# Loading the last piece of the output weight in two DMAs, three rows and then one, in a decode attention kernel

## The chip, the cores and the metric

The kernel runs on one core of one Trainium2 chip. PE is TensorE, DVE VectorE and ACT ScalarE; SP (SyncE) issues the DMAs. A landing is the update of a semaphore by one of the sixteen DMA engines when its share of a transfer has arrived. The metric is the device time of one execution in microseconds (us); the span that the profile shows is some 1.8 us shorter (185.9 for 187.7). A ratio below is the mean time of one kernel's fast runs over that of the other's of the same rounds, so it is not quite the ratio of the medians that are quoted beside it.

## The reference

One decoding step of attention over the last 512 positions of a key and value cache, with 32 query heads on 8 key and value heads, and a projection at each end:

```
q = x @ wq                       # x [32, 1, 512], wq [512, 4096]
k, v = last 512 rows of k_cache, v_cache, each head repeated 4 times
p = softmax(q k^T / sqrt(128))
out = (p v) @ wo                 # wo [4096, 512], bf16
```

The caches' window is 67 MB, wq and wo are 4 MB each. Everything is read once.

## The kernel before

SP issues all large loads in one order: wq, the tiles of K and V (2 MB each), then wo in eight pieces of 512 KB. A piece holds 512 rows of wo; each of the 128 partitions takes four neighbour rows, which are 4 KB in one run of memory. The pieces lie where wq and parts of the attention's data were before, so they wait for a PV stage (the product p v of the reference) to be done with that memory, and come last in the queue:

```python
sp.wait_ge(pe_PV, 2 * Z_HOME.rindex("w") + 2)
for hg in range(NHG):                                  # NHG = 8
    sp.dma_start(
        wo_sb[:, hg].rearrange("p i n -> p (i n)"),
        wo[hg * 512:(hg + 1) * 512, :].rearrange("(m i) n -> m (i n)", i=4),
    ).then_inc(sem_wo[hg], 16)
sp.wait_ge(dve_out, 2)
sp.wait_ge(act_out, 2)
sp.dma_start(out..., out_sb...).then_inc(sem_out, 16)
```

PE takes the pieces in the same order. Each piece is sixteen matmuls: four rows for each partition (i), four column groups (c) that share the array:

```python
for hg in range(NHG):
    pe.wait_ge(sem_wo[hg], 16)
    for i in range(4):
        for c in range(4):
            ins = pe.matmul(
                X_ps[32 * c:32 * (c + 1), 2, 0:128],
                lhsT=o_sel[:, i, hg, :],
                rhs=wo_sb[:, hg, i, c * 128:(c + 1) * 128],
                start=(hg == 0 and i == 0), stop=(hg == NHG - 1 and i == 3),
                tile_position=(0, 32 * c),
            )
ins.then_inc(pe_fin, 1)
```

After the last matmul DVE and ACT copy two quarters of the result each, and SP stores it.

Of the kernel before, what the change touches and what calls it, by code (L numbers as in the profile page):

```python
# [12 lines left out]
def bass_standalone__sliding_block_cached__sampling_kernel(  # L13
# [7 lines left out]
):  # L21
    B, Sq, D = x.shape
    _, HKV, SK, DH = k_cache.shape
    HD = wq.shape[1]
    HQ = HD // DH
# [16 lines left out]
    NHG = HQ // 4  # L42
    NBG = 4 * G
    SELCUT = B - 8
    RING = 3
    XD = 20
    ZD = XD // 4
    ZA = (NBG - XD) // 4
    DMA_ORDER = (
# [21 lines left out]
    with ExitStack() as es:  # L71
        sb = lambda name, shape, dt: es.enter_context(nc.sbuf_tensor(name, shape, dt))
        ps = lambda name, shape, dt: es.enter_context(nc.psum_tensor(name, shape, dt))
        sem = lambda name: es.enter_context(nc.semaphore(name))
# [7 lines left out]
        P_bf = sb("P_bf", [P, KS, KR], BF16)  # L82
        PTc = sb("PTc", [P, RING, KR, REP], BF16)
        pick = sb("pick", [P, REP, KS + P], BF16)
# [20 lines left out]
        wo_sb = w_sb[:, :, :].rearrange("p k n -> p (k n)").rearrange("p (g i n) -> p g i n", g=NHG, i=4)  # L105
# [14 lines left out]
        sem_x = sem("sem_x")  # L120
        sem_wq = [sem(f"sem_wq{i}") for i in range(2)]
        sem_wo = [sem(f"sem_wo{i}") for i in range(NHG)]
        sem_k = [sem(f"sem_k{i}") for i in range(NK)]
        sem_v = [sem(f"sem_v{i}") for i in range(NV)]
        sem_out = sem("sem_out")
# [45 lines left out]
        def z_of(q):  # L171
            return {"w": Z_w, "k": Z_k, "t": Z_t}[Z_HOME[q]]

        def z_waits(eng, q):
            if q == 0:
                eng.wait_ge(pool_mask, 3)
                eng.wait_ge(pe_q, 1)
            elif Z_HOME[q] in Z_HOME[:q]:
                eng.wait_ge(pe_PV, 2 * Z_HOME[:q].rindex(Z_HOME[q]) + 2)
            elif Z_HOME[q] == "k":  # L180
                eng.wait_ge(dve_T, 2 * NCH - 2)
            else:
                eng.wait_ge(pe_S, NQUAD)

        def cache_rows(cache, m):
            q, e = divmod(m, 2)
            rows = cache[4 * q:4 * q + 4, :, SK - W:, :].rearrange("b g (s r) d -> (b g) s (r d)", s=KS)
            return rows[:, :, e * CR * DH:(e + 1) * CR * DH]

        @block.sync  # L190
        def _(sp):
            sp.dma_start(
                w_sb[:, 2:4, :].rearrange("p k n -> p (k n)"), wq_rows[:, wq_half:]
            ).then_inc(sem_wq[1], 16)
            for name in DMA_ORDER:
                n = int(name[1:])
                if name[0] == "K":
                    if n >= NK:
                        sp.wait_ge(dve_T, 2 * (n - NK + 1))
                    sp.dma_start(  # L200
                        K_sb[:, n % NK].rearrange("p r d -> p (r d)"), cache_rows(k_cache, n)
                    ).then_inc(sem_k[n % NK], 16)
                else:
                    if n >= NV:
                        sp.wait_ge(pe_PV, n - NV + 1)
                    sp.dma_start(
                        V_sb[:, n % NV].rearrange("p r d -> p (r d)"), cache_rows(v_cache, n)
                    ).then_inc(sem_v[n % NV], 16)
            sp.wait_ge(pe_PV, 2 * Z_HOME.rindex("w") + 2)
            for hg in range(NHG):  # L210
                sp.dma_start(  # L211
                    wo_sb[:, hg].rearrange("p i n -> p (i n)"),
                    wo[hg * 512:(hg + 1) * 512, :].rearrange("(m i) n -> m (i n)", i=4),
                ).then_inc(sem_wo[hg], 16)
            sp.wait_ge(dve_out, 2)
            sp.wait_ge(act_out, 2)
            sp.dma_start(
                out.rearrange("b s n -> b (s n)"), out_sb[:, :, :].rearrange("b c n -> b (c n)")
            ).then_inc(sem_out, 16)
            sp.wait_ge(sem_out, 16)  # L220
# [58 lines left out]
        def _(pe):  # L279
# [104 lines left out]
            for hg in range(NHG):  # L384
                pe.wait_ge(sem_wo[hg], 16)
                for i in range(4):
                    for c in range(4):
                        ins = pe.matmul(
                            X_ps[32 * c:32 * (c + 1), 2, 0:128],
# [5 lines that stand above are left out]
# [3 lines left out]
        def _(dve):  # L398
# [44 lines left out]
            def spread(q, part):  # L443
# [3 lines left out]
                for k in range(ZD * part, ZD * (part + 1)):  # L447
                    ins = dve.tensor_scalar(  # L448
                        z_of(q)[:, k].rearrange("p x r -> p (x r)"),
                        PTc[:, q % RING].rearrange("p x r -> p (x r)"),  # L450
                        mask[:, k:k + 1], None, op0=ALU.mult,
# [25 lines left out]
        def _(act):  # L477
# [23 lines left out]
            def pt_evac(q):  # L501
                act.wait_ge(pe_PT, q + 1)
                if q >= RING:
                    act.wait_ge(dve_Z, q - RING + 1)
                    act.wait_ge(act_Z, q - RING + 1)
                act.activation(  # L506
                    PTc[:, q % RING], PT_ps[:, :, :].rearrange("p r x -> p x r"), ACTF.Copy
                ).then_inc(act_PT, 1)

            def spread(q, part):  # L510
                if part == 0:
                    act.wait_ge(act_PT, q + 1)
                    z_waits(act, q)
                for k in range(XD + ZA * part, XD + ZA * (part + 1)):
                    ins = act.activation(  # L515
# [57 lines left out]
```

## Time and profile before

| | before |
|---|---|
| time, median of the first 3 runs | 187.70 us (187.68 to 187.76) |
| span of the profiled run | 185.9 us |
| DMA engines, mean rate over the span | 408 GB/s |
| last landing of wo | 182.90 us |
| last matmul's end | 183.38 us |

How to read it: DMA is busy all through, the compute engines are not. The page's lines on DMA add what kinds of packets there are (the counts "under" a size include the semaphore packets of 4 bytes) and, for the issues, how many there were, their size and the median us from issue to landing:

```profile
DMA packets 6160, 75.80 MB, mean 408 GB/s; under 512 B 704, under 2 KB 768, under 8 KB 1792
...
w_sb<-in_wo_dram SPq DMA_DIRECT2D x8, 512.0 KB, 20.3
```

The 1792 less 768 are the 1024 packets of 4 KB of wo: 8 pieces, 128 partitions.

### The profile page before, as it was taken

To read this page: it belongs to the slowest core of one execution; us is meant where nothing else is said; L and a number is where in the kernel's file an instruction comes from. 1 tells how busy PE (TensorE), PEld (TensorE's weight loads), DVE (VectorE), ACT (ScalarE), POOL (GpSimd) and SP (SyncE) were. 2 spreads that over 40 slices of the span, in tenths; PEclk is the share of its full clock that TensorE was granted. 3 is DMA by queue.
4 is the path that set the end of the run, shared out by engine and by line. 5 is a ranking of instruction groups with operands and counts; after the bars stand their busy time and mean duration, and the time that the engine had idled before them with its cause. 6 is when DMAs were issued, how large, how long until landed. Compare 5 with 4: busy or idle time off the path is not lost.

```text
span 185.9 us, 3841 instructions
## 1 busy us (share of the span) xinstructions
PE 110.3 (59%) x1604; PEld 90.7 (49%) x1604; DVE 131.8 (71%) x239; ACT 82.4 (44%) x142; POOL 32.1 (17%) x82
## 2 busy tenths in 40 slices
PE   0232004346179925949726992459699975999851
PEld 0100001032069804929326881129669974999741
DVE  0006999689999799985899959999999993010001
ACT  3001000259420199011992039826989999711011
POOL 7100390500700071050420060000030000000000
PEclk9999999999999995796955899657999999699999
DMA  6999999999999999999999999999999999999980
GB/s 208 419 444 423 430 430 419 444 423 426 426 419 430 426 419 430 434 419 434 418 430 430 423 434 412 441 430 416 432 416 430 423 430 426 423 430 404 401 326 25
DMA packets 6160, 75.80 MB, mean 408 GB/s; under 512 B 704, under 2 KB 768, under 8 KB 1792
## 3 DMA queue, kind: packets, MB, share of 16 engines
q1 hardware_dynamic: 6096, 75.53, 96.2%
q8 instruction: 12, 0.20, 0.4%
q10 hardware_dynamic: 48, 0.03, 0.1%
q14 instruction: 4, 0.03, 0.0%
HBM read 75.53 MB, written 0.03 MB: 406 GB/s over the span
## 4 chain that ended last, share of the span: by engine, by line
DMA 58%; DVE 22%; PE 11%; issue 4%; SPq 3%; ACT 0%; DVEq 0%
DMA V_sb<-in_v_cache_dram 31%; DVE KT_sb L426 14%; DMA w_sb<-in_wo_dram 12%; DMA K_sb<-in_k_cache_dram 8%; PE O_ps L353 7%; DMA w_sb<-in_wq_dram 6%; DVE w_sb L448 4%; DVE QA_sb L416 2%; PE S_ps L316 2%; SPq L211 2%; PE X_ps L296 1%; PE PT_ps L335 1%; SPq L200 1%; DVE oT_sb L409 0%; DVE KT_sb L404 0%
## 5 line engine op out<-in xcount | busy, mean ns | idle before, releaser
L426 DVE STREAM_TRANSPOSE KT_sb<-K_sb 128x2048 uint32<-128x2048 uint32 x32 | 72.3, 2287 | 1.2 <-DMA K_sb<-in_k_cache_dram 1.1
L353 PE MATMUL O_ps<-w_sb,V_sb 128*128 128x128 bf16 x640 | 46.1, 241 | 10.5 <-DMA V_sb<-in_v_cache_dram 5.6
L353 PEld LDWEIGHTS O_ps<-w_sb,V_sb 128*128 128x128 bf16 x640 | 44.7, 109 | 13.7 <-issue 7.0
L265 POOL COPY QBD<-QA_sb 32x64 bf16<-32x64 bf16 x64 | 25.6, 540 | 79.6 <-PE S_ps L316 62.0
L515 ACT ACTIVATE w_sb<-PTc,mask 128x512 bf16<-128x512 bf16 x60 | 38.9, 729 | 0.0
L316 PE MATMUL S_ps<-KT_sb,QBD 128*32 128x512 bf16 x256 | 20.9, 479 | 26.3 <-DVE KT_sb L426 19.8
L448 DVE TENSOR_SCALAR w_sb<-PTc,mask 128x512 bf16<-128x512 bf16 x100 | 30.2, 370 | 4.9 <-PE O_ps L353 4.9
L316 PEld LDWEIGHTS S_ps<-KT_sb,QBD 128*32 128x32 bf16 x256 | 7.8, 110 | 35.9 <-issue 32.0
L487 ACT ACTIVATE X_ps<-S_ps,negmax 128x512 f32<-128x512 f32 x8 | 5.3, 659 | 42.2 <-DVE negmax L435 42.2
L335 PE MATMUL PT_ps<-P_bf,pick 128*128 128x128 bf16 x128 | 11.8, 265 | 18.0 <-ACT P_bf L496 14.7
L335 PEld LDWEIGHTS PT_ps<-P_bf,pick 128*128 128x128 bf16 x128 | 10.2, 122 | 20.9 <-ACT P_bf L496 16.3
L525 ACT ACTIVATE oT_sb<-O_ps 128x128 bf16<-128x128 f32 x8 | 6.0, 750 | 26.0 <-PE O_ps L353 26.0
L515 ACT ACTIVATE K_sb<-PTc,mask 128x512 bf16<-128x512 bf16 x24 | 15.3, 717 | 1.6 <-DVE KT_sb L426 1.6
L353 PE MATMUL O_ps<-K_sb,V_sb 128*128 128x128 bf16 x256 | 15.1, 217 | 1.3 <-DMA V_sb<-in_v_cache_dram 1.0
L353 PEld LDWEIGHTS O_ps<-K_sb,V_sb 128*128 128x128 bf16 x256 | 14.5, 96 | 2.1 <-issue 1.3
L448 DVE TENSOR_SCALAR K_sb<-PTc,mask 128x512 bf16<-128x512 bf16 x40 | 12.1, 377 | 0.3 <-ACT PTc L506 0.2
L353 PE MATMUL O_ps<-KT_sb,V_sb 128*128 128x128 bf16 x128 | 9.1, 240 | 2.4 <-DMA V_sb<-in_v_cache_dram 2.4
L353 PEld LDWEIGHTS O_ps<-KT_sb,V_sb 128*128 128x128 bf16 x128 | 8.9, 108 | 2.5 <-issue 2.5
L469 DVE CAST K_sb<-S_ps 128x256 bf16<-128x256 f32 x1 | 0.4, 424 | 12.7 <-PE S_ps L365 12.7
L515 ACT ACTIVATE KT_sb<-PTc,mask 128x512 bf16<-128x512 bf16 x12 | 7.8, 725 | 0.0
L467 DVE CAST K_sb<-X_ps 128x384 bf16<-128x384 f32 x1 | 0.6, 558 | 9.8 <-PE X_ps L365 9.8
L496 ACT ACTIVATE P_bf<-X_ps,recip 128x512 bf16<-128x512 f32 x8 | 5.5, 685 | 4.4 <-DVE recip L441 4.4
(41 smaller groups left out, 49.5 us busy)
## 6 DMA issues: line engine op xcount, KB each, us to landing
K_sb<-in_k_cache_dram SPq DMA_DIRECT2D x16, 2048.0 KB, 15.2
V_sb<-in_v_cache_dram SPq DMA_DIRECT2D x16, 2048.0 KB, 17.0
w_sb<-in_wq_dram SPq DMA_DIRECT2D x2, 2048.0 KB, 9.7
w_sb<-in_wo_dram SPq DMA_DIRECT2D x8, 512.0 KB, 20.3
oT_sb<-in_x_dram ACTq DMA_DIRECT2D x1, 32.0 KB, 4.5
out_dram<-oT_sb SPq DMA_DIRECT2D x1, 32.0 KB, 1.5
```

The source lines that it names most:

```text
L211: sp.dma_start(wo_sb[:, hg].rearrange("p i n -> p (i n)"), wo[hg * 512:(hg + 1) * 512, :].rearrange("(m i) n -> m (i n)", i=4),).then_inc( ...
L265: pool.tensor_copy(dst[:, i, :, x0:x0 + 4], src).then_inc(pool_qbd, 1)
L316: ins = pe.matmul(S_ps[32 * c:32 * c + 32, q % 2, :], lhsT=QBD[:, q % 2, g, b, e, :], rhs=bass.AP(tensor=KT_sb, offset=s0 * slot + (b * G ...
L335: ins = pe.matmul(PT_ps[:, r, :], lhsT=pick[:, r, KS - s:KS - s + P], rhs=P_bf[:, s, :], start=(s == 0), stop=(s == KS - 1), tile_position ...
L353: ins = pe.matmul(O_ps[:, q % 2, 0:P], lhsT=V_sb[:, m % NV, r, :], rhs=z_of(q)[:, :, x0 + r, :], start=(e == 0 and r == 0), stop=(e == 1 a ...
L416: dve.tensor_copy(QA[32 * a:32 * a + 32, c], QW[32 * c:32 * c + 32, :, :, a::4].rearrange("p h k q -> p h q k"),).then_inc(dve_q, 1)
L426: dve.transpose(KT_w[:, n % NK, b].rearrange("p i r s -> p r i s"), K_w[:, n % NK, :, 32 * b:32 * b + 32],).then_inc(dve_T, 1)
L448: ins = dve.tensor_scalar(z_of(q)[:, k].rearrange("p x r -> p (x r)"), PTc[:, q % RING].rearrange("p x r -> p (x r)"), mask[:, k:k + 1], N ...
L487: act.activation(P_f32, S_ps[:, q % 2, :], ACTF.Exp, bias=negmax[:, q:q + 1], scale=SCALE, accum_out=sums[:, q:q + 1],).then_inc(act_exp, 1)
L496: act.activation(P_bf[:, :, :], P_f32.rearrange("p (x s) -> p s x", s=KS), ACTF.Copy, scale=recip[:, q:q + 1],).then_inc(act_P, 1)
L515: ins = act.activation(z_of(q)[:, k].rearrange("p x r -> p (x r)"), PTc[:, q % RING].rearrange("p x r -> p (x r)"), ACTF.Copy, scale=mask[ ...
L525: act.activation(oT_sb[:, :, 4 * q:4 * q + 4].rearrange("p h a -> p a h"), O_ps[:, q % 2, 0:P].rearrange("p (a h) -> p a h", a=4), ACTF.Co ...
```

## The change

The intent is to leave less for PE to do after the last byte has landed. The last piece comes as three rows for each partition (384 KB), then one row (128 KB) under a semaphore of its own. PE works on the first three rows while the last one is still coming. The constant `WO_CUT = 3` and the semaphore `sem_last` are new; the rest is this:

```diff
             for hg in range(NHG):
-                sp.dma_start(
-                    wo_sb[:, hg].rearrange("p i n -> p (i n)"),
-                    wo[hg * 512:(hg + 1) * 512, :].rearrange("(m i) n -> m (i n)", i=4),
-                ).then_inc(sem_wo[hg], 16)
+                for i0, i1 in ((0, 4),) if hg < NHG - 1 else ((0, WO_CUT), (WO_CUT, 4)):
+                    sp.dma_start(
+                        wo_sb[:, hg, i0:i1].rearrange("p i n -> p (i n)"),
+                        wo[hg * 512:(hg + 1) * 512, :].rearrange("(m i) n -> m (i n)", i=4)[:, i0 * 512:i1 * 512],
+                    ).then_inc(sem_last if i0 else sem_wo[hg], 16)
 ... (PE)
                 for i in range(4):
+                    if hg == NHG - 1 and i == WO_CUT:
+                        pe.wait_ge(sem_last, 16)
```

More of the change, by code (lines that the diff above doesn't have):

```diff
@@ L45, in bass_standalone__sliding_block_cached__sampling_kernel @@
     RING = 3
+    WO_CUT = 3
     XD = 20
@@ L122, in bass_standalone__sliding_block_cached__sampling_kernel @@
         sem_wo = [sem(f"sem_wo{i}") for i in range(NHG)]
+        sem_last = sem("sem_last")
         sem_k = [sem(f"sem_k{i}") for i in range(NK)]
```

## The prediction

> **What bounds the kernel now.** I read the page's slices first, then the chain that ended last, then the timeline of the last microseconds, then busy time by stretch over the same microseconds.
>
> The slices say that the DMA engines are full from the second slice to the last but one, at some 420 GB/s, whatever the compute engines do:
>
> ```profile
> DMA  6999999999999999999999999999999999999980
> GB/s 208 419 444 423 430 430 419 444 423 426 426 419 430 426 419 430 434 419 434 418 430 430 423 434 412 441 430 416 432 416 430 423 430 426 423 430 404 401 326 25
> ```
>
> So the kernel is a stream of 75.5 MB, and its end is the landing of the last piece in that stream plus what has to follow it. The end of the chain shows which piece, and what follows (columns: start us, length us, what):
>
> ```profile
> 159.94 22.96 DMA w_sb<-in_wo_dram
> 182.90 0.04 issue
> 182.94 0.44 PE X_ps L388 x16
> 183.38 0.02 issue
> 183.40 0.28 DVE oT_sb L472
> 183.68 0.31 DVEq L71
> ```
>
> The last piece of wo (512 KB) lands at 182.90; then sixteen matmuls, two evictions and the store of the result run one after the other, and the span closes at 185.9. The change touches the first two of these links alone. The timeline shows how PE lives in that stretch:
>
> ```profile
> 180.48 0.41 PE L388 MATMUL X_ps<-w_sb,K_sb 128*32 128x128 bf16 x16 [0.51 <-DMA w_sb<-in_wo_dram]
> 181.70 0.41 PE L388 MATMUL X_ps<-w_sb,K_sb 128*32 128x128 bf16 x16 [0.82 <-DMA w_sb<-in_wo_dram]
> 182.94 0.41 PE L388 MATMUL X_ps<-w_sb,K_sb 128*32 128x128 bf16 x16 [0.83 <-DMA w_sb<-in_wo_dram]
> ```
>
> The last three pieces come 1.22 and 1.24 us apart, PE needs 0.41 us for each and is idle 0.83 us before each: it waits for the landing and for nothing else. The stretches say how few DMA engines are still at it (columns: busy us of PE, PEld, DVE, ACT, POOL, then the granted clock, the DMA share and GB/s):
>
> ```profile
> 179.00:180.00 1.00, 0.97 (x72) 0.80 (x60) 0.00 (x0) 0.00 (x0) 0.00 (x0) 1.00 0.76 303
> 181.00:182.00 1.00, 0.30 (x16) 0.23 (x16) 0.00 (x0) 0.00 (x0) 0.00 (x0) 1.00 0.21 86
> 182.00:183.00 1.00, 0.17 (x12) 0.06 (x8) 0.00 (x0) 0.00 (x0) 0.00 (x0) 1.00 0.06 25
> ```
>
> A share of 0.06 is one engine of sixteen. The records of single landings in the trace agree: of the sixteen engines' shares of the last piece, thirteen have landed by 181.66, the other three at 182.68, 182.89 and 182.90. So the last landing is set by one or two slow engines, each of which carries 8 rows of 4 KB of every wo piece, one behind the other. I therefore reckon with one engine, not with 420 GB/s.
>
> **What the Trainium skill says.** (1) "DMA: Bandwidth & Descriptors", section "Why a DMA increments its semaphore by 16 and not by 1": each engine that takes part adds one to the semaphore behind its own data, and only the full 16 means that all has landed. The trace agrees: PE starts at 182.94, after the sixteenth update at 182.90, although thirteen were there 1.24 us earlier. (2) The same page, "Why small descriptors are slow (HBM only)": a fixed overhead of about three cycles for each packet. The trace allows a check. On one engine that works alone the packets of 4096 bytes follow each other every 155.4 ns, those of 16384 bytes every 611 ns; the difference is 455.6 ns for 12288 bytes, so 0.0371 ns a byte, and 155.4 - 4096 x 0.0371 leaves 3.5 ns of fixed cost. It is as small as the page says. (3) "Perfetto Trace Analysis", "DMA Optimizations": transfers under 2 KB have significant overhead, and splitting may let work start sooner where the engines are idle. Here both apply at once: the new last packets have 1 KB. The trace speaks against a large overhead: the 1 KB packets of the result's store and of the load of x mostly take 44 to 47 ns. (4) "Runtime: NRT & Kernel Launch", "Instruction fetch mechanics": instructions come in blocks of 16 KB by the sequencer's own DMA queue. The trace has twelve such packets, each of 1.01 to 1.10 us on one engine. Between landings just before and just after those at about 151.8, 163.2 and 171.8 us, one more engine each time is behind the rest by about 1 us more. These are the likely makers of the three stragglers, which is my inference.
>
> **The change part by part.**
>
> *Bytes and issues.* The last 512 KB go as 384 KB (three rows of wo, 3 KB for each partition) and 128 KB (one row, 1 KB). The bytes and the engines stay. Added are one DMA issue on SP, 8 packets and one semaphore packet for each engine, and one wait on PE; nothing is removed.
>
> *Landing of the last byte.* On the slow engine: before, 8 packets of 155.4 ns and one semaphore packet of about 6 ns, so 1.249 us (measured from the slowest landing of one piece to that of the next: 1.24). After, 8 packets of 3 KB at 3072 x 0.0371 + 3.5 = 117.5 ns, a semaphore packet of 6, 8 packets of 1 KB at 41.5 ns, a semaphore packet of 6: 0.940 + 0.006 + 0.332 + 0.006 = 1.284 us. The last landing comes 0.035 us later, at about 182.94. The 384 KB land 0.34 us before it, at about 182.60.
>
> *PE.* Twelve matmuls (three rows, four column groups each) start at about 182.64. Windows cut through the last group show how it fills: the first 4 matmuls are over 0.24 us after the start, 8 after 0.29, 12 after 0.35, 16 after 0.41. So the twelve are through at about 182.99, and have been issued by about 182.84, ahead of the last landing: they lie wholly beside the transfer. After the last landing 4 matmuls are left, 0.24 us in place of 0.41. The term is -0.17 us. It can't be more by this change, as most of the 0.24 is the way of one matmul through the array (219 ns is the record of each).
>
> *The extra wait on PE.* It stands before the four and is already being waited at when the last semaphore comes; the old wait in front of the sixteen had the same place on the path. 0.
>
> *The extra issue on SP.* An issue of wo takes 0.43 us, but the eighth took 8.57 us, from 159.94 to 168.51: something in the queue was full. The ninth may have to wait likewise, for one more 2 MB piece of V to land (V's last two land at 167.9 and 172.8). That puts it at some 173.4 us. The fastest engine gets to the last rows at about 179. The slack is over 5 us, so 0 on the path.
>
> *What follows.* The evictions, the store and the 1.8 us between the span (185.9) and the time (187.7) stay.
>
> *Sum:* +0.035 - 0.17 = -0.135 us. 187.70 - 0.135 = 187.565, told as 187.57 us.
>
> **Rivals.**
>
> *The small packets cost much more than 41.5 ns.* For it: in the load of x some first packets of 1 KB took 179 to 361 ns, and the skill warns of transfers under 2 KB. Against it: those are the first in an empty queue, and the ones behind them took 44 to 47; here the queue is full. If each of the eight took 75 ns, the landing would be 0.27 us later on top, and the time 187.83.
>
> *The ninth issue is late and leaves a gap.* For it: the 8.57 us issue. Against it: the slack above. If it did come after 182.6, the last row would need its whole way from issue to landing, of which the shortest here is the store's 1.5 us: about 189.2. A chance of some 3 in 100.
>
> *The gain is hidden by the stragglers moving.* The end hangs on which engines carry the late instruction fetches. Twelve whole fetches serve PE's stream, and the change adds a single instruction near its end, so the fetches ahead should stay where they are. If one fetch went to another engine, the end would move by up to 1 us either way: 186.6 to 188.6. For it: any new instruction or semaphore could shift the program. A chance of 4 in 100.
>
> *Nothing at all.* If the 4 matmuls took as long as the 16 after a wait (the array filling anew), the time would be 187.74. Against it speaks the 0.24 us of the first four in the same group.
>
> **Range and chances.** The sum has an uncertainty of about 0.06 us in its two terms. The three runs before lie within 0.08 us, and another session or chip may shift by about as much. This gives 187.57 with 187.40 to 187.75 for 8 in 10. A change of 2% is 3.75 us, more than all that follows the last landing (3.0 us), so faster by over 2% is nearly out of the question: 0.005. Slower by over 2% needs a stall larger than any named here: 0.005. Within 2%: 0.99.
>
> **What would show it.** In the changed profile: PE idle once more between a group of 12 and a last group of 4 of L388; the last group some 0.24 us long; about 0.3 us between the two landings; the page's packets under 2 KB up by 128 plus 16 semaphore packets; the distance from the last landing to the span's end down from 3.0 to about 2.85 us. The step on packets is wrong if the last landing is over 0.1 us later than before. The step on SP is wrong if the DMA share falls to 0 before the last landing. The whole prediction is wrong if the set of engines that land after the others changes, which would show as a move of all wo landings by 0.3 us or more.

## The result

The changed kernel took 187.62 us (median of 6 runs, 187.49 to 187.99), the kernel before 187.75 us (median of 6, 187.68 to 187.95). The ratio is 0.9995 with a 95% interval from 0.9982 to 1.0008: the same. The difference of the medians, 0.13 us, is what was predicted, but with single runs that spread over 0.5 us the times alone can't show that it is more than chance. The profile can, because it shows the few links that the change touches.

First the slices of the changed kernel, DMA share and GB/s. They are as before, up to noise:

```profile
DMA  6999999999999999999999999999999999999980
GB/s 194 434 448 412 437 423 423 448 412 437 420 416 441 416 427 434 416 437 427 423 421 423 441 423 420 434 423 430 428 412 434 427 423 430 420 423 411 405 332 27
DMA packets 6304, 75.80 MB, mean 408 GB/s; under 512 B 720, under 2 KB 912, under 8 KB 1936
```

The packets under 2 KB went from 768 to 912: 128 packets of 1 KB and 16 semaphore packets. Of the last microsecond ahead of the last landing there is, as before, only a small share (0.09 here, 0.06 before):

```profile
182.00:183.00 1.00, 0.45 (x24) 0.18 (x12) 0.00 (x0) 0.00 (x0) 0.00 (x0) 1.00 0.09 31
```

That is the work of three engines: by the packet records they write until 182.46, 182.50 and 182.51, and nothing moves after that, as these records end 0.4 to 0.5 us ahead of the landings.

Then the end of the chain (start us, length us, what) and PE's timeline of the last two pieces:

```profile
182.67 0.04 issue
182.71 0.59 PE X_ps L393 x16
183.30 0.02 issue
183.32 0.28 DVE oT_sb L477
```

```profile
181.75 0.41 PE L393 MATMUL X_ps<-w_sb,K_sb 128*32 128x128 bf16 x16 [0.82 <-DMA w_sb<-in_wo_dram]
...
182.71 0.56 PE L393 MATMUL X_ps<-w_sb,K_sb 128*32 128x128 bf16 x16 [0.55 <-DMA w_sb<-in_wo_dram]
```

The chain merges the last sixteen matmuls into one piece that begins at 182.71. It looks longer than before (0.59 for 0.44 us), but it begins earlier against the stream, and it holds a wait. Windows cut at the two landings take it apart (columns as in the prediction):

```profile
182.67:182.99 0.32, 0.28 (x12) 0.18 (x12) 0.00 (x0) 0.00 (x0) 0.00 (x0) 1.00 0.00 0
182.99:183.30 0.31, 0.28 (x12) 0.10 (x4) 0.00 (x0) 0.00 (x0) 0.00 (x0) 1.00 0.00 0
```

Between the two landings PE loads twelve weights, after the second one four. The rest of PE's time in the second window is the end of the twelve, which by their records were still in the array.

A fixed point is needed to compare the two profiles, as the whole stream comes some hundredths or tenths earlier or later from run to run. The landing of the seventh piece serves, as nothing up to it is changed. In the trace's records of landings, the slowest engine's share of each piece came, in us:

| | seventh piece | three rows | last of wo | last matmul's end | seventh to end |
|---|---|---|---|---|---|
| before | 181.66 | | 182.90 | 183.38 | 1.72 |
| changed | 181.71 | 182.67 | 182.99 | 183.30 | 1.59 |

So the last byte comes 1.28 in place of 1.24 us after the seventh piece, and the last matmul ends 0.31 in place of 0.48 us after the last byte: +0.04 and -0.17, together -0.13 us. The ends of matmuls are modelled by the profile, but the copy on DVE, which waits for the last one, says the same: it begins 0.50 us after the last landing before (183.40) and 0.33 us after it here (183.32). There is one profile of before; of the changed kernel there is a second in e1.

### The profile page after: what moved, and what is told of

It is laid out like the page before. It is cut to its first block, busy times and chain, and to the rows that moved or that the text cites. A ratio compares the mean times of both kernels' runs of the same rounds, so it can differ in the third digit from the quotient of the medians.

```text
span 185.9 us, 3842 instructions
## 1 busy us (share of the span) xinstructions
PE 109.0 (59%) x1604; PEld 89.4 (48%) x1604; DVE 131.9 (71%) x239; ACT 82.3 (44%) x142; POOL 32.0 (17%) x82
## 4 chain that ended last, share of the span: by engine, by line
DMA 64%; DVE 20%; PE 9%; issue 3%; SPq 3%; DVEq 0%
DMA V_sb<-in_v_cache_dram 31%; DMA K_sb<-in_k_cache_dram 14%; DMA w_sb<-in_wo_dram 12%; DVE KT_sb L431 12%; PE O_ps L356 8%; DMA w_sb<-in_wq_dram 6%; DVE w_sb L453 4%; DVE QA_sb L421 2%; SPq L214 2%; PE X_ps L299 1%; SPq L202 1%; DVE oT_sb L414 0%; DVE KT_sb L409 0%; PE X_ps L393 0%; DVE maxv L438 0%
## 5 line engine op out<-in xcount | busy, mean ns | idle before, releaser
L356 PE MATMUL O_ps<-w_sb,V_sb 128*128 128x128 bf16 x640 | 47.0, 244 | 9.6 <-DVE w_sb L453 5.0
L356 PEld LDWEIGHTS O_ps<-w_sb,V_sb 128*128 128x128 bf16 x640 | 45.6, 110 | 12.3 <-DVE w_sb L453 6.5
L356 PE MATMUL O_ps<-KT_sb,V_sb 128*128 128x128 bf16 x128 | 7.5, 217 | 2.3 <-DMA V_sb<-in_v_cache_dram 2.3
L356 PEld LDWEIGHTS O_ps<-KT_sb,V_sb 128*128 128x128 bf16 x128 | 7.3, 96 | 2.5 <-issue 2.5
L409 DVE CAST KT_sb<-X_ps 128x512 bf16<-128x512 f32 x1 | 0.7, 692 | 9.2 <-PE X_ps L299 9.2
```

The source lines that it names most:

```text
L356: ins = pe.matmul(O_ps[:, q % 2, 0:P], lhsT=V_sb[:, m % NV, r, :], rhs=z_of(q)[:, :, x0 + r, :], start=(e == 0 and r == 0), stop=(e == 1 a ...
```

## The experiments

All kernels gave correct results. The kernel before ran beside them on the same chip. Experiments e1 to e8 were made on one chip and share its runs of before: median 187.89 us over the 11 runs beside the first set (e1 to e4), and 187.86 over 12 for the second (e5 to e8), which are the same 11 and one more; they lie between 187.59 and 188.30. That is a wider spread than the result's, and the second set is compared almost wholly with runs that were made some minutes earlier. All single runs here count as in the fast state; e9 and e10 are one run each, on another chip, of unknown state.

My theory was the sum in the prediction: two small terms at the end of the stream, and nothing else. The main rivals: packets of 1 KB or a further DMA cost much more; the wait comes back in another form; the late instruction blocks decide.

### e1: the changed kernel again

> The changed kernel once more, as the control of this set. My theory: 0.135 us less than before, so a ratio of 0.9993, too small to be told from 1 by five rounds in which single runs spread over 0.2 to 0.5 us. In the profile, from the slowest landing of the seventh wo piece to the end of the last matmul: 1.59 us (before: 1.72). Rival (a wait has taken the place of the work removed): 1.70 us or more.

Measured: 187.61 us (187.47 to 188.35), ratio 0.9989, interval 0.9973 to 1.0005. The end of its chain:

```profile
182.74 0.59 PE X_ps L393 x16
183.33 0.02 issue
```

The seventh piece landed at 181.73, so the distance to the last matmul's end is 1.60 us, as predicted. The two landings of the last piece came at 182.70 and 183.01, 1.28 us after the seventh. The profile repeats to 0.01 us what the times can't resolve.

### e2 and e5: the split transfer without the gain on PE

```diff
-                    if hg == NHG - 1 and i == WO_CUT:
+                    if hg == NHG - 1 and i == 0:
                         pe.wait_ge(sem_last, 16)
```

> The split transfer alone: PE waits for both parts before the last sixteen matmuls, so nothing is gained on PE. My theory: landing of the last row 1.28 us after the slowest landing of the seventh piece (before 1.24), then the whole group of 0.41 us again: 1.76 us from that landing to the last matmul's end, 0.04 above before and 0.17 above the change. Time within 0.1 us of before. Rival (the second DMA costs a fixed amount of its own, such as a gap of some tenths of a us between two DMAs): a last landing 0.2 us or more later.

Measured: 188.38 us (187.79 to 188.54), ratio 1.0018, interval 1.0003 to 1.0032. The time is 0.5 us above before, where 0.04 was expected. The end of the chain:

```profile
168.63 14.89 DMA w_sb<-in_wo_dram
183.52 0.14 issue
183.66 0.43 PE X_ps L393 x16
```

Two things are new. PE starts 0.14 us after the landing, not 0.04. And the last landing is at 183.52, although fifteen engines had landed by 183.04, as the theory says (1.29 us after the seventh piece at 181.745). In the packet records an instruction block of 16 KB begins at 181.38 right where one engine has just finished its data and has its semaphore packet yet to write; that packet appears at 182.46. The records don't name the engine, so this is a fit of times. It also explains a part only: a landing follows its semaphore packet by 0.41 to 0.49 us in the profiles here, so this packet, which is ahead of the last one (182.62), should have landed at about 182.9 and delayed nothing; it landed 1.06 us after its start. What held it is not shown. I took the block for the cause of the slow runs and ran the kernel again.

> The kernel of e2 once more. Its profile in e2 showed one landing of the last row at 183.52, 0.48 us behind the other fifteen (183.04), and in the packet records the twelfth instruction block of 16 KB on that engine ahead of its last semaphore packet. Theory (collision): five of six runs of e2 were slow by this, and the profiled run and the single runs here fall again into two groups, near 187.8 without the collision and near 188.4 with it; in a profile without it the last landing is 1.28 to 1.31 us after the seventh piece's and the last matmul ends 1.76 us after that. Rival (waiting for two semaphores costs 0.5 us by itself): all runs near 188.4 and in each profile a gap between the last landing and the last group of matmuls.

Measured: 188.03 us (187.69 to 188.70), ratio 1.0009, interval 0.9991 to 1.0028. In this profile nothing is in the way of the last landing:

```profile
183.17 0.14 issue
183.30 0.43 PE X_ps L393 x16
```

The last landing is 1.28 us after the seventh piece (181.89), as the theory has it: a second DMA in a full queue costs 0.04 us and no fixed gap. The rival of e2 falls. But the 0.14 us are there again. In this kernel both waits stand in front of one matmul, and the profile counts 3843 instructions where the changed kernel has 3842: one wait became an instruction of its own on PE. In the trace it is the wait for the last row (at 183.20, 51 ns); the weight load behind it (183.27) holds the wait for the other part, which had long been met. This costs 0.10 us on the path. That it would cost nothing with the two waits in the other order was not tried. With this my sum for this kernel is 0.04 + 0.10 = +0.14 us, and the profile has 1.85 us from the seventh piece to the last matmul's end, 0.13 more than before. The expectation had missed that term. The single runs (187.69, 187.89, 188.03, 188.03, 188.40, 188.70) don't fall into the two groups that the collision theory asked for.

### e6 and e7: the instruction blocks moved

32 small matmuls, 64 instructions with their weight loads, at the start of PE's work; in e6 on the kernel of e2, in e7 on the changed kernel:

```diff
+            for _ in range(32):
+                pe.matmul(S_ps[:, 1, 0:32], lhsT=x_sb...[:, 0], rhs=ident[:, :], start=True, stop=True, ...)
             for kt in range(DKT):
```

> The kernel of e2 with 32 small matmuls more at the start of PE's work, where it waits for wq anyway. Together with their weight loads they are 64 instructions, so every later 16 KB boundary of PE's stream is passed 64 instructions earlier. Theory (collision): the last instruction block, recorded at 180.6 to 181.9 us so far, moves to about 178 us, away from the last semaphore packets; the last landing is no longer delayed, and the time is 187.8, about 0.5 us below e5. If the block comes to one of the three slowest engines instead, the end is later by about 1 us. Rival (two waits): no change against e5. Rival (PE's first work is on the path): longer by some tenths.

> The changed kernel with the same 32 small matmuls in front. Theory (collision): as the last block is out of the way, no run near 188.3 as seen once in e1 (188.35), and the median stays at 187.6, within 0.1 us; the distance from the seventh piece's slowest landing to the last matmul's end stays at 1.59 us. If the block comes to one of the three slowest engines: about 1 us longer. Rival (no influence of instruction blocks): same spread as before, with single runs near 188.3.

Measured: e6 188.21 us (187.96 to 188.67), ratio 1.0017, interval 1.0000 to 1.0035; e7 187.81 us (187.66 to 188.63), ratio 0.9998, interval 0.9981 to 1.0015. The twelfth block did move, to 178.6 us in e6 and 178.0 in e7. The times did not fall, and e7 has a slow single run too (188.63). But the test can't clear the collision of them, as it has a flaw that I had not foreseen: the longer stream needs one block more, and it comes at 182.3 and 181.5 us, as late as the twelfth had come before. What the profiles show is that a run can be slow without it: those of e5 (188.03 us) and e6 (188.25) have no late last landing, but a seventh piece that came at 181.89 and 182.02, 0.2 to 0.4 us later than in before. The queue of instructions on the pages of e7 and of before:

```profile
q8 instruction: 13, 0.21, 0.5%
```

```profile
q8 instruction: 12, 0.20, 0.4%
```

Why single runs of several of these kernels, that before among them, are some 0.5 us above the others stays open. In the profiles the links agree: e6 has 1.85 us from the seventh piece to the last matmul's end like e5, e7 has 1.60 like e1.

The two runs do show one thing, on the late engines. These are the landings of the seventh piece that came last, in us, from the trace's records, with the fastest of the sixteen for comparison:

```
            fastest   then the last five
before      178.37    180.22 180.43 | 181.43 181.65 181.66
changed     178.43    180.24 180.54 | 181.59 181.69 181.71
e6          178.30    180.74 | 181.40 181.66 181.67 182.02
e7          178.32    180.46 | 181.33 181.38 181.56 181.73
```

With one more instruction block ahead of the landing there are four late engines in place of three. That fits the inference in the prediction, that each block holds one engine back by about 1 us, and it speaks against the same three engines being slow in themselves in every run.

### e3: the packet cost made large

Each of the first seven pieces as rows 0 and 2, then rows 1 and 3, so that every packet has 1 KB:

```diff
+                src = wo[...].rearrange("(m i) n -> m i n", i=4)
+                for rows in (slice(0, 4, 2), slice(1, 4, 2)) if hg < NHG - 1 else (slice(0, 4),):
+                    sp.dma_start(wo_sb[:, hg, rows], src[:, rows]).then_inc(sem_wo[hg], 16)
 ... (PE)
-                pe.wait_ge(sem_wo[hg], 16)
+                pe.wait_ge(sem_wo[hg], 32 if hg < NHG - 1 else 16)
```

> The packet cost made large: each of the first seven wo pieces goes as rows 0 and 2, then rows 1 and 3, so in packets of 1 KB and two DMAs; the last piece as before. My theory: a piece takes 32 x 41.5 + 2 x 6 = 1340 ns on the slow engine in place of 1249, so the seven add 0.64 us: time 188.35, ratio 1.0034. Rival (small packets are dear, 75 ns each): a piece takes 2.41 us, the seven add 8.1 us, time 196. Rival (small packets cost nothing at all): 187.7. The 7 issues more on SP should cost nothing: no stretch of 1 us between 160 and 178 with a DMA share under 0.9.

Measured: 189.36 us (189.10 to 189.61), ratio 1.0075, interval 1.0061 to 1.0089: 1.47 us above before, over twice my 0.64, and far from the rival's 8.1. The same window of both kernels, e3 first:

```profile
174.00:176.00 2.00, 2.00 (x40) 2.00 (x37) 0.00 (x0) 0.00 (x0) 0.00 (x0) 1.00 1.10 348
```

```profile
174.00:176.00 2.00, 2.00 (x39) 2.00 (x37) 0.00 (x0) 0.00 (x0) 0.00 (x0) 1.00 1.02 408
```

The engines are full in both (a share a little over 1 is to be read as full), but move 348 in place of 408 GB/s. From slowest landing to slowest landing a piece took 1.50 us while all engines were busy (second to fifth piece, 175.85 to 180.36), which is (1.503 - 0.012) / 32 = 46.6 ns a packet; the seventh, with few engines left, took 1.34 us (181.75 to 183.09), which is the 41.5 ns of the prediction. So the figure was right for a stretch with few engines left, which is the state of the last piece, and too low for a full machine. (Both stretches read the rows in the same pattern, so the pattern is not the difference.) The first pieces here are loaded in the full state; there my expectation went wrong. The fifteen issues on SP cost nothing: of the stretches of 2 us between 160 and 178 us none has a DMA share under 0.96. The stretches of 1 us that the expectation named go down to 0.87, but in before they go down to 0.88 as well, so that limit was too fine. The profiled run was the slowest of the six (189.61), and only 1.44 us of its length come from the seven pieces (seventh landing 183.09 for 181.66): its last piece, which is as before, took 1.53 us in place of 1.24, because beside the three late engines, through by 184.32, one more landed at 184.63 (an instruction block of 1.10 us from 181.88 fits that), and its last sixteen matmuls ran at a granted clock of 0.50 (0.65 us on the chain for 0.44).

### e4: four rows, four DMAs

```diff
+                for i0, i1 in ((0, 4),) if hg < NHG - 1 else ((0, 1), (1, 2), (2, 3), (3, 4)):
+                    sp.dma_start(... i0:i1 ...).then_inc(sem_row[i0 - 1] if i0 else sem_wo[hg], 16)
 ... (PE)
+                    if hg == NHG - 1 and i:
+                        pe.wait_ge(sem_row[i - 1], 16)
```

> The last piece as four rows, each with its own DMA and semaphore: the split carried on. My theory: last landing 4 x (8 x 41.5 + 6) = 1.35 us after the seventh piece's slowest (before 1.24, change 1.28), and the last group of four matmuls ends 0.31 us after it as in the change: 1.66 us to the last matmul's end, so 0.07 worse than the change and 0.06 better than before. Time within 0.1 us of before. Rival (each further DMA in the queue costs some tenths): 2.0 us or more.

Measured: 187.84 us (187.47 to 188.00), ratio 0.9990, interval 0.9976 to 1.0004.

```profile
183.33 0.04 issue
183.37 0.27 PE X_ps L392 x4
183.64 0.02 issue
```

The seventh piece landed at 181.97, so the last landing is 1.35 us behind it and the last matmul's end 1.67 us, both as the sum says. Four matmuls after a landing, alone in the chain here, are the 0.27 us that the change leaves. Splitting on loses 0.07 us to packets and gains nothing, as four matmuls are left either way.

### e8 and e9: the cut after the first row

```diff
-    WO_CUT = 3
+    WO_CUT = 1
```

> The cut after the first row: one row, then three. My theory: the landing is as in the change (1.28 us after the seventh piece's slowest), but twelve matmuls are left, 0.35 us in place of 0.24: 1.28 + 0.04 + 0.35 + 0.02 = 1.70 us to the last matmul's end, against 1.59 for the cut after three and 1.72 before. Time within 0.1 us of before. Rival (only the first matmul's way counts, not how many follow): 1.59 us.

Measured: 187.75 us (187.59 to 187.96, 5 runs), ratio 0.9990, interval 0.9977 to 1.0004. The landing was as expected, 1.29 us after the seventh piece's. But the last twelve matmuls took long, and the stretch shows why:

```profile
183.09 0.51 PE L393 MATMUL X_ps<-w_sb,K_sb 128*32 128x128 bf16 x12 [0.69 <-DMA w_sb<-in_wo_dram]
```

```profile
183.00:183.50 0.50, 0.41 (x12) 0.24 (x12) 0.00 (x0) 0.00 (x0) 0.00 (x0) 0.50 0.00 0
```

The granted clock (the share of TensorE's full clock that the chip allows at that time; the number behind the five busy times) was 0.50.

> The cut after the first row once more, for one look: in the profile of e8 the last twelve matmuls ran at a granted clock of 0.5 and took 0.51 us, so it does not say what twelve cost. My theory: at a granted clock of 1.0 they take 0.35 us and end 0.41 us after the last landing; at 0.5 they take 0.51 us again. Rival (half the clock has nothing to do with it): 0.51 us at full clock as well.

Measured: one run, 187.70 us beside 187.99 for one of before; the profile was at full clock:

```profile
182.94 0.35 PE L393 MATMUL X_ps<-w_sb,K_sb 128*32 128x128 bf16 x12 [0.68 <-DMA w_sb<-in_wo_dram]
```

```profile
183.00:183.50 0.50, 0.29 (x12) 0.11 (x12) 0.16 (x1) 0.16 (x1) 0.00 (x0) 1.00 0.00 0
```

0.35 us for twelve, and 1.69 us from the seventh piece (181.62) to the last matmul's end: between the 1.59 of the change and the 1.72 of before. So it does matter how many matmuls are left, by the amounts read from the group before. And the clock that happens to be granted in the last half microsecond moves the end by 0.16 us (0.51 less 0.35), more than the whole change; e3's last sixteen agree (0.62 us on the timeline at 0.50, for 0.41).

### e10: which engines are late

The last row as DMAs of 112, 8, 4, 2, 1 and 1 partitions, each with its own semaphore; PE waits for all six.

> Which DMA engines are the late ones: the last row goes as DMAs of 112, 8, 4, 2, 1 and 1 partitions, each with its own semaphore. The skill's page on DMA, section on the increment by 16, says that a DMA on n partitions uses the lowest-numbered n engines (for 8, 4, 2 and 1), so the landings of the part of 8 partitions show how late engines 0 to 7 are, and those of 4, 2 and 1 engines 0 to 3, 0 and 1, and 0. Theory (instruction blocks go round the engines): some of the three late engines are above number 7, so fewer than three landings of the part of 8 partitions are 1 us behind. Rival (a fixed group of low-numbered engines takes the instruction blocks): all three are among engines 0 to 7. The time should be within 0.5 us of before; PE waits for six semaphores, at some 0.1 us each.

Measured: one run, 187.96 us beside 187.99 for one of before. Of the part of 8 partitions, five engines landed by 181.01, one at 182.13 and two at 183.11 and 183.13; of the part of 4 the latest was 182.31. If the numbering is as "DMA: Bandwidth & Descriptors", "Why a DMA increments its semaphore by 16 and not by 1", has it (no record here names an engine), two of the three late engines are among 4 to 7, none among 0 to 3, and one is above 7. That is for blocks spread over the engines, and against a group of low-numbered ones that takes them all. It is one run. Its six waits were not 0.1 us each: three became instructions of their own, and the four matmuls began 0.09 us after the last landing, 0.05 more than in the change. I had thought of giving the late engines less of wo, but only the lowest-numbered engines can be chosen by the number of partitions, and they hold late ones too; I didn't build it.

None of the other kernels beats the change in the profile's distance from the seventh piece to the end.

## Why the prediction was right, point by point

**The bound.** Right. The stream and its last landing set the end in every profile here; the distance from the seventh landing to the last matmul's end was changed by what was done to the last pieces and, beside that, by a late last landing in e2 and e3, and by the half clock in e3 and e8. One reading was wrong without harm: the prediction takes a share of 0.06 for one engine, but the packet records show three engines at work until 182.25, 182.42 and 182.49; the share is an average over a microsecond of which they fill less than half. (PE's idle time before the first of its three lines is 0.51 us, too, not 0.83.)

**The last landing, +0.035 us.** Measured +0.040 (1.281 against 1.241 us from the seventh piece), e1 +0.043. The packets of 1 KB have their own cost of 41.5 ns only where few engines are left; e3 shows 46.6 ns in a full machine. In the changed kernel's records they follow each other every 42 to 43 ns, and the packets of 3 KB every 118 ns. The estimate mixed two states: the 155.4 ns for 4 KB come from the end, with three engines left, the 611 ns for 16 KB from the middle of the stream, with all of them busy. The sizes of the end alone give (155.4 - 42.5) / 3072 = 0.0368 ns a byte and about 5 ns a packet in place of 3.5; over eight more packets that is 0.01 us. And the page's warning of transfers under 2 KB ("Perfetto Trace Analysis", "DMA Optimizations") is of DMAs of that size, while this one has 128 KB in packets of 1 KB; no run here tests it.

**Twelve matmuls beside the transfer, -0.17 us.** Measured: 0.48 us from last landing to last matmul before, 0.31 after. e4 shows four matmuls alone, e9 twelve; both agree with the way the old group of sixteen filled. One sign did not come as forecast: PE is not idle between the twelve and the four in the records, as the last of the twelve end at 183.06 and the four begin at 183.03; the gap is in the weight loads. From last landing to the span's end it is 3.05 us before and 2.91 after. The interval between the two landings was 0.32 us, predicted 0.34.

**The extra wait on PE, 0.** Right for the change, where each wait is in front of its own matmul. e2, e5 and e6 show that this hangs on the place: two waits in front of one matmul cost 0.10 us.

**The extra issue on SP, 0 on the path.** The conclusion held, the way to it did not. I expected the ninth issue at some 173.4 us, after one more piece of V. It went at 168.5, right behind the eighth, which had been held until then as before, and took 1.95 us; that is still some 9 us ahead of the fastest engine's end of the three rows (179.42). What the queue had been full of is not settled, but it is not simply a number of DMAs: in e3, where a DMA has 16 packets of data for each engine in place of 8, it was the fifth issue that was held (8.51 us, until 168.5). My check for this step was badly put too: the share of the DMA in a window falls to zero before the last landing in both kernels, because the packets' records end 0.4 to 0.5 us ahead of the landing's. The packets themselves follow each other without a gap up to 182.50.

**The late engines.** Three are late after the change, as before; whether they are the same three the records don't tell. e6 and e7 support their cause, the instruction blocks. That a block can reach one more engine and move the end, as the prediction's rival of the stragglers had it, e3's profile makes likely (0.3 us). The late last landing of e2's profile cost 0.5 us, and I had not thought of that way; that the block beside it is the whole cause, and that it slows many runs, is not shown.

**The sum, -0.135 us, and the time, 187.57 us.** The medians differ by 0.13 us and the changed kernel's is 187.62, inside the stated range. In the profile the sum is -0.13 and in e1 -0.12. The interval of the ratio includes 1, so the gain rests on the profiles and not on the times. That the medians differ by just the predicted amount is luck: in e1 they differ by 0.28 us. What was right for its own reason is the sum of the two terms.

## What to carry to other kernels

When a stream of loads sets the end, only what follows its last byte is worth shortening: cut the last load so that little compute is left behind it, and cut it once, since each further cut makes the stream itself longer (e4). Take the price of small packets from the stretch in which they will run, and give every wait an instruction of its own to stand in front of. A gain of 0.1 us in 188 has to be read as a distance between two events of the profile, as clock and landing times move the total by more than that from run to run.

## What the Trainium skill lacked or had wrong

- "DMA: Bandwidth & Descriptors", "Why small descriptors are slow (HBM only)", gives a fixed overhead of a packet, 27% of the time of one of 256 bytes; of 256 x 0.0371 + 3.5 = 13.0 ns, 3.5 ns are 27% too, so it agrees with the prediction's figure where few engines are left (about 5 ns by the packets of the end alone). It lacks what a packet costs when all engines are busy: by e3, a packet of 1 KB took 46.6 ns, while one of 4 KB in before took 159.7 ns (pieces 1.2835 us apart, less 6 ns, by 8). So three packets more cost 4 x 46.6 - 159.7 = 26.7 ns, or 9 ns each.
- "Runtime: NRT & Kernel Launch", "Instruction fetch mechanics", calls the cost of crossing a block of 16 KB mostly hidden. For the engine that fetches it may be; in this kernel, bound by DMA, each block takes one DMA engine for 1.0 to 1.1 us (before), and it fits that the engines so delayed land last (three of sixteen, 1.0 to 1.2 us behind the thirteenth in before; four of them with one block more, e6 and e7).
- "Perfetto Trace Analysis", "Identifying Dependency Chains", tells that an instruction for a further wait may be put in front, but I found no page that says what it costs: with two waits 0.14 us in place of 0.04 from the landing to the first matmul (e2, e5, e6), with six 0.09 (e10).
- I found no page that says how many issued DMAs can stand in the queue before the issuing sequencer is held: the eighth wo issue took 8.57 us in place of 0.43, in e3 with twice the packets the fifth 8.51.
